# RMS norm inside a fused retention, MLP and gated MLP kernel: means and root rows in two 12-bit parts, diagonals one task earlier

## The chip, the cores and the metric

One core of a Trainium2 chip runs the whole program. The metric is the device time of one execution in microseconds, the median of several runs. The engines of the core work side by side, each through its own list of instructions in order: TensorE (PE; its weight loads are listed as PEld) multiplies matrices into PSUM, ScalarE (ACT) computes functions and copies, VectorE (DVE) does elementwise work, GpSimd (POOL) some of it, and SyncE (SP) issues the transfers. They meet only at semaphores.

## What is computed

Three stages on 1536 tokens of width 512: a retention (linear attention with decay), an MLP with a sigmoid-weighted activation, and an RMS-normed gated MLP. The last one, in which the change lies:

```python
def _moe2_ref(x, w_gate, w_val, w_out, rms_g):
    rms = np.sqrt(np.mean(x * x, axis=-1, keepdims=True) + 1e-06)
    xn = x / rms * rms_g
    g = xn @ w_gate
    silu = g * (1.0 / (1.0 + np.exp(-g)))
    val = xn @ w_val
    return (silu * val @ w_out).astype(np.float32)
```

All of it is in 32-bit floats.

## The kernel before

**Products.** Nearly all large products are made of parts: each factor is split into a high part of 12 bits (a copy by ACT into the type float32r) and the rest (a subtraction by DVE), and `product` (L295) adds three TensorE products, high by high, high by low, low by high. `halves` (L302) makes such a pair. The norm alone still multiplies whole 32-bit floats.

**Tiles and stages.** Tokens lie in three blocks of 512, called 0, 1 and 2 (OTHER, FIRST, LAST). Features lie on the 128 partitions, so a block is 4 tiles of 128 x 512. After the retention comes the first MLP in 48 steps (`STEPS`): step i makes one tile of h (`mlp1_in`, 12 products into one of the two PSUM buffers of the pool `ps_h`), its Silu `g` (`mlp1_act`, ACT, L330), the parts `gh` (ACT) and `gl` (DVE), and one step later 12 products into the four accumulators (`mlp1_out`). `split_in` makes the weight parts `wih`, `wil` two steps ahead into four buffers, `split_out` makes `woh`, `wol` into two; the ACT half waits until TensorE has read the buffer's last content. The second MLP follows as chains (`seven`): products named by output and side, `g0a`, `v0a`, `g0b`, `v0b` and so on, copied and combined by ACT and DVE; finished features go into output products `o`.

**The norm.** When a block is done, `norm_tasks` (L368) gives six tasks, which are handed out one by one between the steps of other work: two with the squares of the four tiles (ACT, L373) and their sum (DVE, L377); one with the means (four TensorE products of the squares with a column of 1/512, L382) and the roots (DVE adds epsilon, ACT takes the square root, L389, DVE the reciprocal and one Newton step, L390 to L394); one with the diagonals (ACT multiplies an identity by each of four columns of roots, L399) and the row of roots (four products of a matrix of ones with them, L407, so that each partition has the root of each token); two in which DVE scales the tiles (L410). Norm 1 is that of block 1 (its means are at 238 us of the trace), norm 2 that of block 0 (262 us), both beside steps 32 to 40 of the first MLP; norm 3, of block 2 (340 us), lies beside the first chains of the second MLP: its squares, means and roots are tasks of the walk through group 0, the rest comes in the walk through group 2.

**What sets the order.** The text of the program gives a first order; while the program is built the instructions of each engine are put into one list by their estimated times, so that neighbours of different tasks mix. A square root and a Silu need different tables of ACT; each change is an instruction `ACT_TABLE_LOAD`. Copies work with either. Beside the norms, ACT and DVE convert the weights of the second MLP from 64-bit words (`qw`, `uw`, L146 to L152); the results are stored to DRAM and reloaded (`w20r`, `w21r`, ...) by transfers on SP's queue.

Of the kernel before, what the change touches and what calls it, by code (L numbers as in the profile page):

```python
# [9 lines left out]
F32 = mybir.dt.float32  # L10
F32R = mybir.dt.float32r
U32 = mybir.dt.uint32
U64 = mybir.dt.uint64
ACTF = mybir.ActivationFunctionType
ALU = mybir.AluOpType
# [3 lines left out]
C = 128  # L19
# [7 lines left out]
T = 512  # L27
NB = NT // T
CPB = T // C
EPS = 1e-6  # L30
# [16 lines left out]
def tile_retention_mlp_swiglu(  # L47
# [19 lines left out]
    nc = tc.nc  # L67
    pool = lambda name, bufs, **kw: ctx.enter_context(tc.tile_pool(name=name, bufs=bufs, **kw))
    const = pool("const", 1)
# [20 lines left out]
    sm_sb = const.tile([128, 12, 1], F32, name="sm_sb")  # L90
    g_sb = const.tile([128, KD], F32, name="g_sb")
    ones = const.tile([128, 128], F32, name="ones")
    mean_w = const.tile([128, 1], F32, name="mean_w")
    pad = const.tile([128, 24], F32, name="pad")
    ident = const.tile([128, 128], F32, name="ident")
    nm = {n: const.tile([128, T // C], F32, name=f"nm{n}") for n in "mqrt"}

    def tmp(name):
        return tmp_p.tile([128, T], F32, tag="tmp", name=name)

    def psum(p, name):
        return p.tile([128, T], F32, tag=p.name, name=name)
# [199 lines left out]
    def halves(hi, lo, src):  # L302
        nc.scalar.activation(out=hi, in_=src, func=ACTF.Copy)  # L303
        nc.vector.tensor_tensor(out=lo, in0=src, in1=hi.bitcast(F32), op=ALU.subtract)  # L304
# [17 lines left out]
    def mlp1_in(i):  # L322
        j, f, _, _ = STEPS[i]
        ps = psum(ps_h, f"h{j}_{f}")
        in_proj(ps, parts.pop(("wi", i)), xt[j])
        return ps
# [41 lines left out]
    def norm_tasks(j, p):  # L368
        x, st = x1[j], {}

        def squares(m):
            sq = tmp(f"sq{j}_{m}")
            nc.scalar.activation(out=sq, in_=x[:, m, :], func=ACTF.Square)  # L373
            if m == 0:
                st["s"] = sq
            else:
                nc.vector.tensor_tensor(out=st["s"], in0=st["s"], in1=sq, op=ALU.add)  # L377

        def means():
            st["ps"] = psum(p, f"mean{j}")  # L380
            for i in range(T // C):
                nc.tensor.matmul(  # L382
                    out=st["ps"][:, i:i + 1], lhsT=st["s"][:, i * C:(i + 1) * C], rhs=mean_w, start=True, stop=True
                )

        def roots():
            m, q, r, t = (nm[n] for n in "mqrt")
            nc.vector.tensor_scalar(out=m, in0=st["ps"][:, 0:T // C], scalar1=EPS, scalar2=None, op0=ALU.add)
            nc.scalar.activation(out=q, in_=m, func=ACTF.Sqrt)  # L389
            nc.vector.reciprocal(out=r, in_=q)  # L390
            nc.vector.tensor_tensor(out=t, in0=r, in1=r, op=ALU.mult)
            nc.vector.tensor_tensor(out=t, in0=t, in1=m, op=ALU.mult)
            nc.vector.tensor_scalar(out=t, in0=t, scalar1=-0.5, scalar2=1.5, op0=ALU.mult, op1=ALU.add)
            nc.vector.tensor_tensor(out=r, in0=r, in1=t, op=ALU.mult)  # L394

        def diagonals():
            st["d"] = tmp(f"diag{j}")
            for i in range(T // C):
                nc.scalar.activation(  # L399
                    out=st["d"][:, i * C:(i + 1) * C], in_=ident, func=ACTF.Copy, scale=nm["r"][:, i:i + 1]  # L400
                )

        def rows():
            st["r"] = psum(p, f"r{j}")
            for i in range(T // C):
                o = slice(i * C, i * C + C)
                nc.tensor.matmul(out=st["r"][:, o], lhsT=ones, rhs=st["d"][:, o], start=True, stop=True)  # L407

        def scale(m):
            nc.vector.scalar_tensor_tensor(  # L410
                out=x[:, m, :], in0=st["r"], scalar=g_sb[:, m:m + 1], in1=x[:, m, :], op0=ALU.mult, op1=ALU.mult
            )

        return [
            lambda: (squares(0), squares(1)), lambda: (squares(2), squares(3)), lambda: (means(), roots()),
            lambda: (diagonals(), rows()),
            lambda: (scale(0), scale(1)), lambda: (scale(2), scale(3)),
        ]

# [294 lines left out]
    for i, (j, f, first, last) in enumerate(STEPS):  # L714
# [9 lines left out]
        ps = mlp1_in(i)  # L724
        next_of(att)
        mlp1_act(i, ps)
        if i:
            mlp1_out(i - 1)
            if STEPS[i - 1][3] and STEPS[i - 1][1] == F1 - 1:
                norm += norm_tasks(STEPS[i - 1][0], ps_t)  # L730
                if STEPS[i - 1][0] == OTHER:
                    norm += x_tasks()
# [61 lines left out]
    mlp1_out(len(STEPS) - 1)  # L794
    reload("w3", 0)
    norm = norm_tasks(LAST, ps_a)
    for g in range(0, F2, 2):
        more = g + 2 < F2
# [6 lines left out]
        n = len(work) - 10  # L805
# [108 lines left out]
```

## Time and profile before

| what | value |
|---|---|
| median of 3 runs | 612.28 us (612.24 to 613.17) |
| the profiled execution | 611.25 us, span 609.4 us |
| PE busy | 596.2 us, 98% of the span, 3354 instructions |
| DVE busy | 443.3 us, 73% |
| ACT busy | 357.0 us, 59% |
| mean granted TensorE clock | 0.994 of full speed |
| chain that ended last | PE 86%, DVE 7%, DMA 3%, ACT 2%, issue 2% |

The span is the time from the first to the last instruction on the core; 1.85 us of the execution lie around it. Busy shares are means over stages with different limits. TensorE's products overlap, so that a product of 512 columns lasts 0.39 us but the next can start 0.23 us later; what counts is the distance of the starts. All times of the rows below are microseconds from the start of the span.

### The profile page before, as it was taken

The numbers are of one execution on the slowest core, as the hardware profiler recorded it, in microseconds if no ns is written. First come the engines' busy times: TensorE is split into PE (matmuls) and PEld (weight loads), VectorE is DVE, ScalarE is ACT, GpSimd is POOL, SyncE is SP. The second block draws the span as 40 slices with busy tenths as digits, with TensorE's granted clock in tenths as the row PEclk, the third lists the DMA queues.
The fourth block names the chain that finished last, engine by engine and source line by source line (L and its number), as shares of the span: only waits on it lengthen the run. The fifth ranks groups of instructions, "written<-read, shape, count | busy, mean of one in ns | idle before, by whom it ended". The sixth has DMA issues, their size and how long they took to land.

```text
span 609.4 us, 9229 instructions
## 1 busy us (share of the span) xinstructions
PE 596.2 (98%) x3354; PEld 496.8 (82%) x3354; DVE 443.3 (73%) x791; ACT 357.0 (59%) x657; POOL 39.1 (6%) x36
## 2 busy tenths in 40 slices
PE   7899999999999999999999999999999999999997
PEld 5678888888878888888887788898988889988885
DVE  2799978777797768889997999374565756655542
ACT  1386847676665558877776875354444536544532
POOL 4516010000022100000000000000000000000000
PEclk8899999999999999999999999999999999999999
DMA  8767652334667545427663132021221366643521
GB/s 335 310 208 272 229 186 94 117 136 155 193 205 233 160 146 159 131 73 227 188 194 118 67 106 104 34 89 51 75 99 46 128 235 220 224 152 104 173 70 69
DMA packets 32733, 93.14 MB, mean 153 GB/s; under 512 B 3888, under 2 KB 3888, under 8 KB 32688
## 3 DMA queue, kind: packets, MB, share of 16 engines
q1 hardware_dynamic: 32688, 92.56, 45.9%
q8 instruction: 26, 0.43, 0.3%
q14 instruction: 19, 0.16, 0.1%
HBM read 73.67 MB, written 18.87 MB: 152 GB/s over the span
## 4 chain that ended last, share of the span: by engine, by line
PE 86%; DVE 7%; DMA 3%; ACT 2%; issue 2%; SPq 0%; POOL 0%; DVEq 0%; ACTq 0%; POOLq 0%
PE acc L298 6%; PE acc L299 6%; PE acc L300 6%; PE h L298 6%; PE h L299 6%; PE h L300 6%; PE o L298 5%; PE o L299 5%; PE o L300 5%; PE sc L225 2%; PE y L257 2%; PE y L247 1%; DVE qw L150 1%; DMA sm_sb<-in_small 1%; DMA w23r<-w23d 1%
## 5 line engine op out<-in xcount | busy, mean ns | idle before, releaser
L299 PE MATMUL acc<-gl,woh 128*128 128x512 f32 x192 | 75.2, 391 | 2.2 <-DVE gl L333 2.2
L298 PE MATMUL acc<-gh,woh 128*128 128x512 f32 x192 | 75.9, 399 | 0.1
L300 PE MATMUL acc<-gh,wol 128*128 128x512 f32 x192 | 74.9, 390 | 0.0
L170 ACT ACTIVATE wih<-w 128x512 fp32r<-128x512 f32 x48 | 30.2, 631 | 65.5 <-PE h L299 56.2
L298 PE MATMUL o<-w3h,gh 128*128 128x512 f32 x144 | 56.2, 390 | 0.0
L299 PE MATMUL o<-w3l,gh 128*128 128x512 f32 x144 | 56.2, 390 | 0.0
L300 PE MATMUL o<-w3h,gl 128*128 128x512 f32 x144 | 56.1, 389 | 0.0
L171 DVE TENSOR_TENSOR wil<-w,wih 128x512 fp32r<-128x512 f32 x48 | 32.8, 689 | 24.9 <-ACT wih L170 24.8
L150 DVE CUSTOM_DVE_ANT_0 qw<-qw,uw 128x1024 uint16<-128x1024 uint16 x68 | 49.8, 733 | 0.6
L146 ACT ACTIVATE qw<-w 128x512 f32<-128x512 f32 x68 | 45.1, 663 | 0.4 <-DMA w<-in_w 0.4
L147 ACT ACTIVATE uw<-w 128x512 uint32<-128x512 uint32 x68 | 45.2, 665 | 0.0
L299 PEld LDWEIGHTS acc<-gl,woh 128*128 128x128 f32 x192 | 36.1, 188 | 10.1 <-DVE gl L333 3.1
L298 PEld LDWEIGHTS acc<-gh,woh 128*128 128x128 f32 x192 | 35.9, 188 | 9.0 <-ACT gh L332 0.6
L300 PEld LDWEIGHTS acc<-gh,wol 128*128 128x128 f32 x192 | 36.0, 188 | 7.5
L170 ACT ACTIVATE woh<-w 128x512 fp32r<-128x512 f32 x48 | 30.2, 630 | 12.5 <-PE acc L299 11.7
L149 DVE TENSOR_SCALAR qw<-qw 128x512 uint32<-128x512 uint32 x68 | 30.4, 448 | 8.8 <-ACT qw L146 8.8
L304 DVE TENSOR_TENSOR gl<-gw,gh 128x512 fp32r<-128x512 f32 x24 | 16.6, 692 | 25.9 <-ACT gh L303 25.9
L333 DVE SCALAR_TENSOR_TENSOR gl<-g,gh 128x512 fp32r<-128x512 f32 x48 | 33.4, 696 | 2.5 <-ACT gh L332 1.0
L171 DVE TENSOR_TENSOR wol<-w,woh 128x512 fp32r<-128x512 f32 x48 | 32.9, 685 | 2.8 <-ACT woh L170 2.7
L300 PEld LDWEIGHTS o<-w3h,gl 128*128 128x128 f32 x144 | 27.0, 188 | 5.6
L303 ACT ACTIVATE gh<-gw 128x512 fp32r<-128x512 f32 x24 | 15.1, 631 | 27.6 <-PE o L299 24.8
L299 PEld LDWEIGHTS o<-w3l,gh 128*128 128x128 f32 x144 | 27.1, 188 | 4.7
(1113 smaller groups left out, 1521.2 us busy)
## 6 DMA issues: line engine op xcount, KB each, us to landing
w<-in_w SPq DMA_DIRECT2D x68, 512.0 KB, 4.4
qk<-in_qk SPq DMA_DIRECT2D x12, 512.0 KB, 6.3
kv<-in_kv SPq DMA_DIRECT2D x12, 512.0 KB, 6.6
g0d<-gs SPq DMA_DIRECT2D x12, 256.0 KB, 2.0
g2d<-gl SPq DMA_DIRECT2D x12, 256.0 KB, 2.1
out<-o SPq DMA_DIRECT2D x12, 256.0 KB, 2.4
gw<-g0d SPq DMA_DIRECT2D x12, 256.0 KB, 2.7
gw<-g2d SPq DMA_DIRECT2D x12, 256.0 KB, 2.7
```

The lines of the kernel that those rows point to most:

```text
L146: nc.scalar.activation(out=q, in_=high.bitcast(F32), func=ACTF.Copy, scale=2.0 ** -112)
L147: nc.scalar.activation(out=t, in_=low, func=ACTF.Copy, scale=2.0 ** -29)
L149: nc.vector.tensor_scalar(out=m, in0=m, scalar1=3, scalar2=None, op0=ALU.logical_shift_left)
L150: nc.vector.tensor_tensor(out=m, in0=m, in1=t, op=ALU.add)
L170: nc.scalar.activation(out=hi, in_=src, func=ACTF.Copy)
L171: nc.vector.tensor_tensor(out=lo, in0=src, in1=hi.bitcast(F32), op=ALU.subtract)
L298: nc.tensor.matmul(out=out, lhsT=ah, rhs=bh, start=first, stop=False)
L299: nc.tensor.matmul(out=out, lhsT=ah, rhs=bl, start=False, stop=False)
L300: nc.tensor.matmul(out=out, lhsT=al, rhs=bh, start=False, stop=last)
L303: nc.scalar.activation(out=hi, in_=src, func=ACTF.Copy)
L304: nc.vector.tensor_tensor(out=lo, in0=src, in1=hi.bitcast(F32), op=ALU.subtract)
L333: nc.vector.scalar_tensor_tensor(out=lo, in0=g, scalar=1.0 / GELU, in1=hi.bitcast(F32), op0=ALU.mult, op1=ALU.subtract)
```

## The change

- The sum of squares `s` is split by `halves` into `sh` and `sl` at the end of the second task (`two`).
- The means are eight float32r products instead of four 32-bit ones: for each group of 128 tokens `sh` and `sl` with `mean_w`, which now has two equal columns, added up in PSUM; the epsilon line reads every second column.
- The row of roots is split too: `nmh` and `nml` (128 x 4 each), and two sets of four diagonals, `diagh` and `diagl`. The row is two float32r products over all 512 columns instead of four 32-bit ones of 128.
- The diagonals move from the fourth task into the third, behind the roots; the fourth task holds only the two products.

```diff
--- before.py
+++ after.py
@@ -90,10 +90,10 @@
     sm_sb = const.tile([128, 12, 1], F32, name="sm_sb")
     g_sb = const.tile([128, KD], F32, name="g_sb")
     ones = const.tile([128, 128], F32, name="ones")
-    mean_w = const.tile([128, 1], F32, name="mean_w")
+    mean_w = const.tile([128, 2], F32, name="mean_w")
     pad = const.tile([128, 24], F32, name="pad")
     ident = const.tile([128, 128], F32, name="ident")
-    nm = {n: const.tile([128, T // C], F32, name=f"nm{n}") for n in "mqrt"}
+    nm = {n: const.tile([128, T // C], F32, name=f"nm{n}") for n in "mqrthl"}
 
     def tmp(name):
         return tmp_p.tile([128, T], F32, tag="tmp", name=name)
@@ -376,16 +376,22 @@
             else:
                 nc.vector.tensor_tensor(out=st["s"], in0=st["s"], in1=sq, op=ALU.add)
 
+        def two():
+            st["sh"], st["sl"] = (tmp(f"s{x}{j}").bitcast(F32R) for x in "hl")
+            halves(st["sh"], st["sl"], st["s"])
+
         def means():
             st["ps"] = psum(p, f"mean{j}")
             for i in range(T // C):
-                nc.tensor.matmul(
-                    out=st["ps"][:, i:i + 1], lhsT=st["s"][:, i * C:(i + 1) * C], rhs=mean_w, start=True, stop=True
-                )
+                for x in ("sh", "sl"):
+                    nc.tensor.matmul(
+                        out=st["ps"][:, 2 * i:2 * i + 2], lhsT=st[x][:, i * C:(i + 1) * C], rhs=mean_w.bitcast(F32R),
+                        start=x == "sh", stop=x == "sl",
+                    )
 
         def roots():
             m, q, r, t = (nm[n] for n in "mqrt")
-            nc.vector.tensor_scalar(out=m, in0=st["ps"][:, 0:T // C], scalar1=EPS, scalar2=None, op0=ALU.add)
+            nc.vector.tensor_scalar(out=m, in0=st["ps"][:, 0:2 * T // C].rearrange("p (i two) -> p i two", two=2)[:, :, 0], scalar1=EPS, scalar2=None, op0=ALU.add)
             nc.scalar.activation(out=q, in_=m, func=ACTF.Sqrt)
             nc.vector.reciprocal(out=r, in_=q)
             nc.vector.tensor_tensor(out=t, in0=r, in1=r, op=ALU.mult)
@@ -394,17 +400,20 @@
             nc.vector.tensor_tensor(out=r, in0=r, in1=t, op=ALU.mult)
 
         def diagonals():
-            st["d"] = tmp(f"diag{j}")
-            for i in range(T // C):
-                nc.scalar.activation(
-                    out=st["d"][:, i * C:(i + 1) * C], in_=ident, func=ACTF.Copy, scale=nm["r"][:, i:i + 1]
-                )
+            halves(nm["h"].bitcast(F32R), nm["l"].bitcast(F32R), nm["r"])
+            for s in "hl":
+                st[s] = tmp(f"diag{s}{j}").bitcast(F32R)
+                for i in range(T // C):
+                    nc.scalar.activation(
+                        out=st[s][:, i * C:(i + 1) * C], in_=ident, func=ACTF.Copy, scale=nm[s][:, i:i + 1]
+                    )
 
         def rows():
             st["r"] = psum(p, f"r{j}")
-            for i in range(T // C):
-                o = slice(i * C, i * C + C)
-                nc.tensor.matmul(out=st["r"][:, o], lhsT=ones, rhs=st["d"][:, o], start=True, stop=True)
+            for s in "hl":
+                nc.tensor.matmul(
+                    out=st["r"], lhsT=ones.bitcast(F32R), rhs=st[s], start=s == "h", stop=s == "l"
+                )
 
         def scale(m):
             nc.vector.scalar_tensor_tensor(
@@ -412,8 +421,8 @@
             )
 
         return [
-            lambda: (squares(0), squares(1)), lambda: (squares(2), squares(3)), lambda: (means(), roots()),
-            lambda: (diagonals(), rows()),
+            lambda: (squares(0), squares(1)), lambda: (squares(2), squares(3), two()),
+            lambda: (means(), roots(), diagonals()), rows,
             lambda: (scale(0), scale(1)), lambda: (scale(2), scale(3)),
         ]
```

The built lists show what this moves. The first place is ACT in norm 1, from the load of the square root's table (L389, L395 in the changed file) on. `nmq` is the square root, `nmr` the finished root, `diag` the diagonals, `wih37` a weight part of step 37, `g33` and `gh33` the Silu of step 33 and its high part, `qw261` and `uw261` a weight conversion; the brackets name the engines waited for. Before:

```order
L389 ACT_TABLE_LOAD
L389 ACTIVATE nmq_107<-nmm_106 128x4 [waits DVE_49]
L330 ACT_TABLE_LOAD [waits DMAHW0_49]
L330 ACTIVATE g33_2590<-h2_1_2577 128x512 [waits PE_49]
L399 ACTIVATE diag1_2620<-ident_105,nmr_108 128x128 [waits DVE_49]
L332 ACTIVATE gh33_2592<-g33_2590 128x512 [waits Activation_49]
L399 ACTIVATE diag1_2620<-ident_105,nmr_108 128x128 x3
L146 ACTIVATE qw270_2630<-w270_64_2417 128x512 [waits DMAHW1_49]
```

Changed:

```order
L395 ACT_TABLE_LOAD
L395 ACTIVATE nmq_107<-nmm_106 128x4 [waits DVE_49]
L170 ACTIVATE wih37_2713<-w15_621 128x512 [waits PE_49]
L303 ACTIVATE nmh_110<-nmr_108 128x4 [waits DVE_49]
L407 ACTIVATE diagh1_2571<-ident_105,nmh_110 128x128 [waits DMAHW0_49,Activation_49]
L407 ACTIVATE diagh1_2571<-ident_105,nmh_110 128x128 x3
L407 ACTIVATE diagl1_2576<-ident_105,nml_111 128x128 [waits DVE_49]
L407 ACTIVATE diagl1_2576<-ident_105,nml_111 128x128 x3
L146 ACTIVATE qw261_2581<-w261_64_2350 128x512 [waits DMAHW7_49]
L147 ACTIVATE uw261_2582<-w261_64_2350 128x512 [waits DMAHW0_49]
L330 ACT_TABLE_LOAD
L330 ACTIVATE g33_2612<-h2_1_2599 128x512 [waits PE_49]
```

`wih37`, the eight diagonals and a conversion now stand between the root and the next Silu; before, only that Silu's table load did. On TensorE the first product of h of step 35 waits for ACT in the new list; it writes the PSUM buffer that `g33` reads. On DVE a subtraction `wil37` stands directly ahead of the last step of `nmr`, and four `scale` operations ahead of `gl33`.

The second place is ACT in norm 2, from `nmq` on; `woh38` is a weight part of step 38, `g37` the Silu of step 37. Before:

```order
L389 ACTIVATE nmq_107<-nmm_106 128x4 [waits DVE_49]
L170 ACTIVATE wih41_2937<-w19_933 128x512 [waits PE_49]
L399 ACTIVATE diag0_2806<-ident_105,nmr_108 128x128 [waits DVE_49]
L399 ACTIVATE diag0_2806<-ident_105,nmr_108 128x128 x3
L146 ACTIVATE qw331_2816<-w331_64_2567 128x512 [waits DMAHW7_49]
L147 ACTIVATE uw331_2817<-w331_64_2567 128x512
L330 ACT_TABLE_LOAD [waits DMAHW0_49]
L330 ACTIVATE g37_2847<-h2_5_2834 128x512 [waits PE_49]
```

Changed:

```order
L395 ACTIVATE nmq_107<-nmm_106 128x4 [waits DVE_49]
L170 ACTIVATE wih41_2965<-w19_935 128x512 [waits PE_49]
L170 ACTIVATE woh38_2908<-w16_704 128x512 [waits PE_49]
L303 ACTIVATE nmh_110<-nmr_108 128x4 [waits DVE_49]
L407 ACTIVATE diagh0_2831<-ident_105,nmh_110 128x128 [waits Activation_49]
L407 ACTIVATE diagh0_2831<-ident_105,nmh_110 128x128 x3
L407 ACTIVATE diagl0_2836<-ident_105,nml_111 128x128 [waits DVE_49]
L407 ACTIVATE diagl0_2836<-ident_105,nml_111 128x128 x3
L146 ACTIVATE qw331_2844<-w331_64_2589 128x512 [waits DMAHW7_49,DMAHW0_49]
L147 ACTIVATE uw331_2845<-w331_64_2589 128x512
L330 ACT_TABLE_LOAD
L330 ACTIVATE g37_2875<-h2_5_2862 128x512
```

`woh38`, which waits for TensorE, moved from behind `g37` to ahead of `nmh`. On TensorE the row's products moved from the middle of step 36's output to h of step 38, and the first product of h of step 39 waits for ACT.

The third place is TensorE in norm 3, from the last products of `g0a` and `v0a` that read the sum `wg0y`, `wv0y` on. `wg0z` belongs to the next pair, which adds to the same PSUM tile after ACT has copied it (`rg`). Before (the row came a group later, between products of `v2a` and `g2b`):

```order
L382 MATMUL mean2_3559<-mean_w_103,sq2_0_3498 128x1 [waits DVE_49]
L382 MATMUL mean2_3559<-mean_w_103,sq2_0_3498 128x1 x3
L587 MATMUL g0a_3445<-xh5_3239,wg0yl_3407 128x512
L587 MATMUL v0a_3458<-xh5_3239,wv0yh_3410 128x512 [waits Activation_49]
L587 MATMUL v0a_3458<-xl5_3240,wv0yh_3410 128x512
L587 MATMUL v0a_3458<-xh5_3239,wv0yl_3411 128x512
L587 MATMUL v0a_3458<-xh5_3239,wv0yh_3410 128x512
L587 MATMUL v0a_3458<-xl5_3240,wv0yh_3410 128x512
L587 MATMUL v0a_3458<-xh5_3239,wv0yl_3411 128x512
L587 MATMUL g0a_3445<-xh3_3243,wg0zh_3414 128x512 [waits Activation_49]
```

Changed:

```order
L387 MATMUL mean2_3591<-mean_w_103,sh2_3561 128x2
L387 MATMUL mean2_3591<-mean_w_103,sl2_3562 128x2
L387 MATMUL mean2_3591<-mean_w_103,sh2_3561 128x2
L387 MATMUL mean2_3591<-mean_w_103,sl2_3562 128x2
L387 MATMUL mean2_3591<-mean_w_103,sh2_3561 128x2
L387 MATMUL mean2_3591<-mean_w_103,sl2_3562 128x2
L596 MATMUL v0a_3486<-xl5_3268,wv0yh_3438 128x512
L596 MATMUL v0a_3486<-xh5_3267,wv0yl_3439 128x512
L414 MATMUL r2_3717<-diagh2_3609,ones_102 128x512 [waits Activation_49]
L298 MATMUL o10_3795<-w3h0_3799,gh0_3522 128x512
L414 MATMUL r2_3717<-diagl2_3614,ones_102 128x512 [waits Activation_49]
L596 MATMUL g0a_3473<-xh3_3271,wg0zh_3442 128x512 [waits Activation_49]
```

The row now stands behind the means with two products of `v0a` between, and `g0a` comes after it. On ACT `wv2yh`, a weight part that reuses the buffer of `wv0y`, stands ahead of the square root's table load, and `rg` moved from ahead of that load to behind the eight diagonals. On DVE `sl` is new between the last addition and the means, and `wv0yl` moved ahead of the first operation that needs the reloaded `w23`, with one of the four operations between that one and `gl47` moved behind it (at 325 us of the old trace).

## Rows read from the trace of the kernel before

**Rows 1.** Busy us by stretch: length, PE, PEld, DVE, ACT, POOL; then clock.

```profile
272.00:322.00 50.00, 50.00 (x222) 41.24 (x221) 49.10 (x83) 38.69 (x68) 0.00 (x0) 1.00 0.64 202
...
362.00:500.00 138.00, 138.00 (x726) 118.80 (x725) 85.98 (x169) 63.58 (x125) 0.00 (x0) 1.00 0.26 93
```

**Rows 2.** Waits of TensorE alone: who <- whom, us in total, times, longest.

```profile
PE acc L299 <- DVE gl L333: 2.2, 2, 1.3
```

**Rows 3.** Line 407, the row of roots: times in ns, first and last start.

```profile
L407 PE MATMUL r<-diag,ones x24: 270/275/377, 244.6 to 353.3; 128*128 128x128 f32 x24
```

**Rows 4.** Timeline of TensorE, norm 1: start, duration, what, tile, count.

```profile
241.62 0.39 PE L298 MATMUL acc<-gh,woh 128*128 128x512 f32 x1
...
244.34 0.39 PE L298 MATMUL h<-xt2h,wih 128*128 128x512 f32 x1
...
245.26 0.40 PE L298 MATMUL h<-xt2h,wih 128*128 128x512 f32 x1
...
245.49 0.83 PE L407 MATMUL r<-diag,ones 128*128 128x128 f32 x6
...
246.39 0.39 PE L300 MATMUL h<-xt2h,wil 128*128 128x512 f32 x1
```

**Rows 5.** Timeline of ACT and DVE, norm 1.

```profile
238.57 1.28 ACT L389 ACT_TABLE_LOAD   x1
...
239.86 0.20 ACT L389 ACTIVATE nmq<-nmm 128x4 f32<-128x4 f32 x1
...
241.82 0.60 ACT L330 ACTIVATE g<-h 128x512 f32<-128x512 f32 x1 [0.45 <-PE h L300]
...
242.60 0.16 DVE L394 TENSOR_TENSOR nmr<-nmr,nmt 128x4 f32<-128x4 f32 x1
...
243.63 0.97 ACT L399 ACTIVATE diag<-ident,nmr 128x128 f32<-128x128 f32 x3
...
244.51 0.64 ACT L146 ACTIVATE qw<-w 128x512 f32<-128x512 f32 x1
...
245.06 0.64 ACT L147 ACTIVATE uw<-w 128x512 uint32<-128x512 uint32 x1
```

**Rows 6.** Timeline of ACT and of TensorE's weight loads, norm 2.

```profile
267.12 1.28 ACT L399 ACTIVATE diag<-ident,nmr 128x128 f32<-128x128 f32 x4 [1.24 <-DVE nmr L394]
...
267.57 0.30 PEld L407 LDWEIGHTS r<-diag,ones 128*128 128x128 f32 x2 [0.51 <-ACT diag L399]
...
270.83 0.60 ACT L330 ACTIVATE g<-h 128x512 f32<-128x512 f32 x1
```

**Rows 7.** Timeline of TensorE, ACT and DVE, norm 3.

```profile
340.12 1.05 PE L382 MATMUL mean<-mean_w,sq 128*128 128x1 f32 x8
...
342.17 1.28 ACT L389 ACT_TABLE_LOAD   x1
...
345.33 0.15 DVE L394 TENSOR_TENSOR nmr<-nmr,nmt 128x4 f32<-128x4 f32 x1
...
346.15 0.50 PE L587 MATMUL v0a<-xh,wv0zh 128*128 128x512 f32 x1 [0.53 <-ACT rv L594]
```

**Rows 8.** Timeline of DVE and TensorE around 325.

```profile
322.75 0.42 DVE L501 TENSOR_TENSOR swg<-w23r 128x256 f32<-128x256 f32 x1 [1.58 <-DMA w23r<-w23d]
...
325.44 0.50 PE L299 MATMUL acc<-gl,woh 128*128 128x512 f32 x1 [1.27 <-DVE gl L333]
```

**Rows 9.** Timeline of TensorE at the start of the program.

```profile
18.41 1.09 PE L247 MATMUL y<-qd,S_sb 64*64 64x128 f32 x16
...
23.49 1.12 PE L282 MATMUL u<-kv,kd 128*64 128x64 f32 x16 [2.51 <-POOL kd L212]
...
24.55 1.97 PE L247 MATMUL y<-qd,S_sb 64*64 64x128 f32 x16
```

**Rows 10.** Busy time at the start and behind 325 (columns as above).

```profile
24.00:26.00 2.00, 2.00 (x26) 1.88 (x24) 1.10 (x3) 0.00 (x0) 0.00 (x0) 0.50 1.02 408
...
326.00:328.00 2.00, 2.00 (x10) 1.66 (x9) 2.00 (x6) 1.53 (x3) 0.00 (x0) 1.00 0.35 137
```

## The prediction

> **What bounds the kernel now.** First the busy time by stage: TensorE works through all 50.00 us of 272 to 322 and all 138.00 us of 362 to 500 [rows 1]. Then the list of who waited for whom, TensorE alone: in the middle of the kernel one wait matters, 1.3 us at 325 for `gl` [rows 2, 8]. So the time is TensorE's row of products, and after 362 no gap is left in which a loss could be made good. ScalarE (ACT) is not full, VectorE (DVE) nearly is (49.10 of 50 us before 322 [rows 1]), and both work strictly in the order of their lists, so the timeline around the three norms (blocks 1, 0 and 2, at 238, 262 and 340 us) decides. It shows that the old chain of roots hardly stops TensorE: in norm 1 the row of roots runs between other products without a wait [rows 4], in norm 2 its weight load stood idle for 0.51 us [rows 6], in norm 3 TensorE stood 0.53 us for the copy `rv`, which ACT made late because two table loads lay ahead of it [rows 7].
>
> My sum is made against the profiled execution, 611.25 us (span 609.4 and 1.85 around it); the median of the runs shown lies 1.03 above it.
>
> **Prices.** A product of 512 columns costs 2.72/12 = 0.227 us of TensorE (from 241.62 to 244.34 twelve start [rows 4]). The six short records of the row take (246.39 - 245.26) - 2 x 0.227 = 0.676, or 0.113 each [rows 4]. Successive 512-wide ACT operations start 0.55 apart [rows 5]; a further diagonal costs 1.28 - 0.97 = 0.31 (four against three [rows 5, 6]); a table load 1.28 [rows 5]. Right behind the load `nmq` starts, at 239.86, when the load ends at 239.85 [rows 5]. The Trainium skill (ScalarE: Activation LUTs, What ACT_TABLE_LOAD costs) adds about 1.4 us of drain to each load; by that the sum below would grow by some 7 us (two loads ahead of the Silu in norms 1 and 2, one in norm 3). The trace does not agree, so that case gets no chance.
>
> **The change on TensorE itself.** The row of roots: 8 short records a norm (24 in all [rows 3]) become two full ones: 0.90 - 0.45 = 0.45 us saved a norm. The means: 8 records before, 8 after, with two columns instead of one. No row shows a 12-bit product so narrow; it lies between 0.113 (same weights, more columns) and 0.227 (full width), 0 to +0.9 a norm; I take 0, since the load of 128 weight columns is the same. Sum: -1.36 us. The added ACT and DVE work (`sh`, `sl`, `nmh`, `nml`, four more diagonals: 0.55 + 0.6 + 0.2 + 0.2 + 1.24 us a norm) would lie beside products if it came early; what it costs is where it stands, place by place below. The moved step issues no transfer. Three more of the 14 `tmp` buffers are taken a norm; where a buffer's last user is a store (`diagh` of norm 1 waits for one) that store was issued some 10 us earlier, so 0. The wider `mean_w` is set by GpSimd before the first product, 0.
>
> **Norm 1.** On ACT the eight diagonals, and behind them `qw`, `uw` and the Silu table load, now stand ahead of `g33`, the Silu of step 33 (order, first place). Before, `g33` ran at 241.82 [rows 5]. Now: `nmr` follows on DVE behind `wil37`, which needs `wih37`, which waits for the last reader in h of step 33. That reader starts two products before 241.62, at 241.17, so it ends near 241.56; `wih37` 241.6 to 242.2, `wil37` to 242.9, `nmr` to 243.0 (242.60 before [rows 5]), `nmh` to 243.25, diagonals 243.3 to 245.7 (8 x 0.31), `qw` and `uw` to 246.75, table load to 248.0, `g33` to 248.6. TensorE starts h of step 34 at 244.34 as before [rows 4]; 12 products and 2 for the row end at 247.5. Then h of step 35 wants the PSUM buffer that `g33` still reads (there are two): 1.1 us of standing. Behind it DVE has four `scale` operations ahead of `gl33`: 0.4 more. +1.55 - 0.45 = **+1.1** (0 if `g33` got ready by 247.5; 1.9 with a slow DVE).
>
> **Norm 2.** On ACT `woh38` now stands ahead of `nmh` (second place). It reuses the buffer of step 36, so it waits for TensorE's second-last product of step 36's output. On the old axis: without the row and its wait that product ends at 267.95; `woh38` to 268.5, `nmh` to 268.7, diagonals to 271.2, `qw`, `uw` to 272.3, table load to 273.55, `g37` to 274.15 (270.83 before [rows 6]). TensorE begins h of step 38 at 268.0, 14 products to 271.2, of which the second row product waits 0.35 for its diagonals; h of step 39 then waits for `g37`: 2.6. Saved: the wait of before, 0.35 of the 0.51 [rows 6], and 0.45. **+2.15** (1.0 to 3.0).
>
> **Norm 3.** Here the cover is thinnest: after the means TensorE has two products left before the row (third place). ACT's `sh` and DVE's `sl` come after the last addition, which lets the means go at 340.12 [rows 7]: 340.1 + 0.6 + 0.7 = 341.4. TensorE runs four products meanwhile and loses 0.25; the means end near 342.4. ACT's `wv2yh` now stands ahead of the Sqrt load and waits for a product behind the means (342.8), so the load starts at 343.35 instead of 342.17 [rows 7], `nmr` comes 1.2 to 1.3 later than 345.33 [rows 7], at 346.6, `nmh` 346.85, four diagonals 348.15. TensorE, free at 342.9, stands 5.3 us. Then one product of `o`, 0.7 for the other four diagonals, 0.3 for the copy `rg`, which ACT makes only behind them. 6.55 in all. Saved: 0.45, and some 1.2 of waits of before (0.53 and its restart for `rv`, the rest for the row's diagonals, which stood one by one between products). **+4.9** (3.5 to 6).
>
> **Between.** The stop at 325 came from DVE waiting 1.58 us for the reload of `w23` and running four operations before `gl47` [rows 8]. Now `wv0yl` fills that wait and `gl47` has one operation less ahead of it: **-0.8** (0 to -1.5). Two transfers on SP's queue change places (`w211d` ahead of `w30r`, `w22r`, `w23r`, and `w21r` earlier); the reload of `w23` was released by DVE, not by them, so I give this nothing.
>
> Sum of the places: 1.1 + 2.15 + 4.9 - 0.8 = +7.35.
>
> **The clock.** At the start TensorE stood 2.51 us before 23.49 and then ran at a granted clock of 0.50, the 1.2 GHz level, for all of 24 to 26; sixteen products took 1.97 us where they take 1.09 [rows 9, 10]. The 1.3 us at 325 left the clock at 1.00 [rows 8, 10]. So the 5.3 us of norm 3 should bring it down, the 2.6 us of norm 2 perhaps. Price: the row shows two us at that level; two to four (an estimate, up to twice the row's) of dense work at half pace lose 1 to 2; I take **+1.7** for norm 3. The Trainium skill (TensorE: Matmul & The Clock Gate, What's actually happening) calls the low level the default, which activity lifts; the trace agrees with its 0.50 at 24 us.
>
> 611.25 + 7.35 + 1.7 = 620.3 for a profiled execution, 621.3 for the median.
>
> **The rivals.**
> 1. Three stops, the clock falls after norm 3 (forecast): 621.3, own range 618.5 to 624.
> 2. Three stops and no fall of the clock: 612.28 + 7.35 = 619.6. For it: products go on in small numbers in norm 3.
> 3. The clock falls after norm 2 too, at its 2.6 us, close to the 2.51 that did it at 23.49 [rows 9]: + 1.7, or 623.0; with a longer low stretch 626.
> 4. Only norm 3 stops: `g33` and `g37` come in time because ACT gets through its waits sooner than I have it. Then norms 1 and 2 give -0.45 and -0.8, and the sum is 612.28 - 1.25 + 4.9 - 0.8 + 1.7 = 616.8.
> 5. Faster: the roots are ready when TensorE reaches the row, as "a step ahead" says. Then 1.36 us of records, 0.35 and 1.2 of waits go: 609.4. It decides at one point, norm 3: from the end of the means to four diagonals there would have to pass 0.45 us of TensorE's work, and the old trace needs 345.33 - 341.17 = 4.2 us for the root alone [rows 7]; in norms 1 and 2 the Silu would have to end by 247.5 and 271.5. I see nothing for it.
>
> **How the numbers follow.** Chances: 1: 0.50; 2: 0.18; 3: 0.17; 4: 0.08; 5: 0.04; nothing that can be told from no change (0.2% is about that limit): 0.03. Faster 0.04, same 0.03, slower 0.93. The time is that of case 1, 621.3. The range must take in 2 and most of 3, the end of my bounds below (1.5 less in the places) and half of 4: 616.8 to 625.5.
>
> **What would show it.** In the profile after: TensorE waiting in h for ACT's Silu (L330) near 248 and 275, each behind a table load; one gap of about 5 us near 345 that ends with the row's product on `diagh`; the granted clock at 0.5 in the microseconds behind it; the row as two records of 512 columns; eight narrow records for the means at about 0.11. Wrong would be: no wait on the Silu (then norms 1 and 2 are cheap), a gap in norm 3 under 3 us (then a chain element is shorter than its row), or narrow records of over 0.2.

## The result, and the profile after

The changed kernel takes 621.47 us (median; single executions 619.17 to 622.29) where the kernel before takes 612.26 on the same chip: ratio 1.0144, 95% interval 1.0124 to 1.0165. Forecast were 621.3 and slower. Its profiled execution took 620.87 us with a span of 619.1, 9.7 more than that of before.

The page's first lines: busy time and instructions, then the shares of the chain that ended last.

```profile
PE 598.0 (97%) x3336; PEld 495.9 (80%) x3336; DVE 446.0 (72%) x797; ACT 363.3 (59%) x675; POOL 33.4 (5%) x36
...
PE 84%; DVE 6%; ACT 4%; issue 2%; DMA 2%; POOL 1%; SPq 0%; DVEq 0%; ACTq 0%; POOLq 0%
```

TensorE has 18 instructions less and 1.8 us more busy time; ACT's share of the chain went from 2% to 4%. Why stands in the list of TensorE's waits (who <- whom, us in total, times, longest), where two lines are new:

```profile
PE r L414 <- ACT diagh L407: 5.3, 1, 5.3
PE h L298 <- ACT g L330: 3.6, 2, 2.5
PE acc L299 <- DVE gl L333: 1.3, 2, 1.0
```

The row waits for the diagonals once, 5.3 us (norm 3); h waits for the Silu twice, 3.6 us in all (norms 1 and 2); the wait for `gl` that [rows 2] shows is smaller.

**Norm 1**, timeline (start, duration, engine, what; the idle time before and its releaser in brackets):

```profile
238.58 0.21 ACT L395 ACTIVATE nmq<-nmm 128x4 f32<-128x4 f32 x1
240.31 0.64 ACT L170 ACTIVATE wih<-w 128x512 fp32r<-128x512 f32 x1 [1.52 <-PE h L299]
...
243.21 1.27 ACT L407 ACTIVATE diagl<-ident,nml 128x128 fp32r<-128x128 f32 x4
...
245.60 1.28 ACT L330 ACT_TABLE_LOAD   x1
246.89 0.60 ACT L330 ACTIVATE g<-h 128x512 f32<-128x512 f32 x1
...
247.54 0.50 PE L298 MATMUL h<-xt2h,wih 128*128 128x512 f32 x1 [1.11 <-ACT g L330]
```

The Silu of step 33 ran at 241.82 in [rows 5]; now it stands behind `wih37`, eight diagonals, a conversion and a table load, runs at 246.89, and TensorE stands 1.11 us in h of step 35. No time passes behind a table load: it starts at 245.60, takes 1.28, and the Silu starts at 246.89.

**Norm 2:**

```profile
267.85 0.64 ACT L170 ACTIVATE woh<-w 128x512 fp32r<-128x512 f32 x1 [2.08 <-PE acc L299]
268.38 0.19 ACT L303 ACTIVATE nmh<-nmr 128x4 fp32r<-128x4 f32 x1
...
273.48 0.60 ACT L330 ACTIVATE g<-h 128x512 f32<-128x512 f32 x1
...
274.13 0.50 PE L298 MATMUL h<-xt2h,wih 128*128 128x512 f32 x1 [2.52 <-ACT g L330]
...
275.16 0.56 PE L299 MATMUL h<-xt2l,wih 128*128 128x512 f32 x1
...
278.80 0.40 PE L300 MATMUL acc<-gh,wol 128*128 128x512 f32 x1
```

`woh38` holds ACT idle for 2.08 us until TensorE has read its buffer, and the Silu of step 37 comes at 273.48 instead of 270.83 [rows 6]. TensorE stands 2.52 us, and the clock falls behind it: the nine products from 275.16 to 278.80 take 3.64 us, at 0.227 they would take 2.04. The busy time by stretch says the same (columns as in [rows 1]):

```profile
276.00:278.00 2.00, 2.00 (x6) 1.60 (x5) 2.00 (x5) 2.00 (x5) 0.00 (x0) 0.50 0.82 248
```

**Norm 3**, timeline and then busy time by stretch:

```profile
345.55 0.39 PE L596 MATMUL v0a<-xh,wv0yl 128*128 128x512 f32 x1
...
346.40 1.28 ACT L395 ACT_TABLE_LOAD   x1
...
349.43 0.17 DVE L400 TENSOR_TENSOR nmr<-nmr,nmt 128x4 f32<-128x4 f32 x1
...
351.20 0.79 PE L414 MATMUL r<-diagh,ones 128*128 128x512 f32 x1 [5.26 <-ACT diagh L407]
...
357.23 0.39 PE L596 MATMUL v0a<-xl,wv0zh 128*128 128x512 f32 x1
```

```profile
348.00:350.00 2.00, 0.00 (x0) 0.00 (x0) 1.69 (x10) 0.34 (x2) 0.00 (x0) 0.50 0.34 131
...
354.00:356.00 2.00, 2.00 (x6) 1.52 (x5) 2.00 (x4) 1.40 (x3) 0.00 (x0) 0.50 0.00 0
```

The row stands 5.26 us for `diagh`, the clock is at 0.50 before it ends, and stays there for the products behind it.

**Around 325** (DVE, then TensorE):

```profile
326.50 0.43 DVE L510 TENSOR_TENSOR swg<-w23r 128x256 f32<-128x256 f32 x1 [0.34 <-DMA w23r<-w23d]
...
327.51 0.68 DVE L333 SCALAR_TENSOR_TENSOR gl<-g,gh 128x512 fp32r<-128x512 f32 x1
...
328.25 0.50 PE L299 MATMUL acc<-gl,woh 128*128 128x512 f32 x1 [0.31 <-DVE gl L333]
```

`gl47` now starts 1.01 us after DVE's first use of `w23` (`swg`). Before, where that use was at 322.75 [rows 8], it was 1.95:

```profile
324.70 0.68 DVE L333 SCALAR_TENSOR_TENSOR gl<-g,gh 128x512 fp32r<-128x512 f32 x1
```

Where the 9.7 us lie can be read from four products that every trace has: the first of the means in norm 1, the first of the means in norm 2, the first of `g0a` (behind 325), the first of `g4a` (behind norm 3). How far each comes later than before, and by how much that grew in between:

| | norm 1's means | norm 2's means | `g0a` | `g4a` | span |
|---|---|---|---|---|---|
| before | 237.95 | 261.61 | 328.07 | 374.71 | 609.4 |
| after | 236.66 | 261.50 | 330.90 | 384.77 | 619.1 |
| later by | -1.29 | -0.11 | 2.83 | 10.06 | 9.7 |
| grown by | start: -1.29 | norm 1: +1.18 | norm 2 and 325: +2.94 | norm 3: +7.23 | rest: -0.4 |

### The profile page after: what moved, and what is told of

It is laid out like the page before. It is cut to its first block, busy times and chain, and to the rows that moved or that the text cites. A ratio compares the mean times of both kernels' runs of the same rounds, so it can differ in the third digit from the quotient of the medians.

```text
span 619.1 us, 9214 instructions
## 1 busy us (share of the span) xinstructions
PE 598.0 (97%) x3336; PEld 495.9 (80%) x3336; DVE 446.0 (72%) x797; ACT 363.3 (59%) x675; POOL 33.4 (5%) x36
## 4 chain that ended last, share of the span: by engine, by line
PE 84%; DVE 6%; ACT 4%; issue 2%; DMA 2%; POOL 1%; SPq 0%; DVEq 0%; ACTq 0%; POOLq 0%
PE acc L298 6%; PE acc L299 6%; PE acc L300 6%; PE h L298 6%; PE h L299 6%; PE h L300 6%; PE o L298 5%; PE o L299 5%; PE o L300 5%; PE sc L225 2%; PE y L257 2%; PE y L247 1%; DMA sm_sb<-in_small 1%; PE g10a L596 1%; PE g8a L596 1%
## 5 line engine op out<-in xcount | busy, mean ns | idle before, releaser
L298 PEld LDWEIGHTS o<-w3h,gh 128*128 128x128 f32 x144 | 27.2, 189 | 4.7
```

The source lines that it names most:

```text
L298: nc.tensor.matmul(out=out, lhsT=ah, rhs=bh, start=first, stop=False)
```

## The experiments

The same reading for each kernel that ran, from its profiled execution (us; the last two columns are the stop of TensorE at 325 for `gl`, and the ratio to the kernel before on the same chip with its 95% interval):

| kernel | start | norm 1 | norm 2 and 325 | norm 3 | stop at 325 | ratio |
|---|---|---|---|---|---|---|
| changed kernel | -1.29 | +1.18 | +2.94 | +7.23 | 0.31 | 1.0144 (1.0124 to 1.0165) |
| undo_third | +0.35 | +1.17 | +3.06 | +0.31 | 0.32 | 1.0049 (1.0030 to 1.0069) |
| parts_only | +1.28 | -0.45 | +4.90 | +0.31 | 0.30 | 1.0065 (1.0040 to 1.0090) |
| move_only | -1.13 | +0.01 | +0.01 | +5.14 | 1.66 | 1.0050 (1.0030 to 1.0071) |
| mean_parts | -0.01 | -0.01 | +2.34 | +0.70 | 2.44 | 0.9995 (0.9978 to 1.0012) |
| fill_gap | +0.78 | +1.20 | +2.69 | +3.43 | 0.30 | 1.0128 (1.0098 to 1.0159) |
| pool_diag | +0.12 | +4.74 | +4.53 | +8.15 | 0.33 | 1.0291 (1.0259 to 1.0324) |
| move_rows | -0.17 | +1.18 | -0.15 | +4.86 | 0 | 1.0088 (1.0064 to 1.0111) |
| nodiag32 | -0.03 | -0.02 | -0.16 | -0.88 | 1.06 | 1.0001 (0.9978 to 1.0025) |
| nodiag_parts | -0.96 | -0.03 | +0.15 | -0.16 | 0.72 | 1.0021 (0.9998 to 1.0044) |
| late_only | +1.05 | -0.04 | +0.43 | +0.05 | 1.75 | 1.0003 (0.9980 to 1.0026) |
| nodiag_late | +1.50 | -0.02 | -0.96 | -0.88 | 0.26 | 0.9959 (0.9944 to 0.9975) |

Up to the means of norm 1 the programs are nearly the same; what differs there, from -1.29 to +1.50, is mostly how one execution differs from another. Ratios rest on 4 to 12 executions each, columns on one, and that one need not be typical: for mean_parts it is the slowest of ten (614.62 us), for nodiag_late the slowest of twelve (610.87), for nodiag_parts the fastest of ten (610.31).

**undo_third: the changed kernel, norm 3 alone put back.**

```
-            lambda: (means(), roots(), diagonals()), rows,
+            lambda: (means(), roots(), diagonals()) if j != LAST else (means(), roots()),
+            lambda: rows() if j != LAST else (diagonals(), rows()),
```

> The changed kernel with one thing undone: in norm 3 alone the diagonals go back into the fourth task. Everything up to 325 us keeps the order of the changed kernel. Theory of places: the 5.3 us stop ahead of the row in norm 3 and the low clock behind it vanish, and with them the 7.1 us by which the offset between the two traces grows there (2.83 at the end of the first MLP, 9.98 at the third pair of chains). 621.5 - 7.2 = 614.3, range 613.3 to 615.5. Rival, the extra work in 12-bit parts costs wherever it stands: only the diagonals' place changes, the work does not, so the time stays above 619.

614.79 us: the stop and the low clock behind it are gone, norm 3 costs 0.31 instead of 7.23 and norms 1 and 2 cost what they did. So the work in parts is not what costs in norm 3, its place is. The 0.31 has a new wait of 0.94 for `qg` at the first `g2a` in it, while the wait for `rv` [rows 7] is gone; mean_parts, which has the same two and keeps the 32-bit row, shows 0.70, and the row in parts saves 0.45 of that.

**parts_only: the move undone in all three norms.**

```
-            lambda: (means(), roots(), diagonals()), rows,
+            lambda: (means(), roots()), lambda: (diagonals(), rows()),
```

> The changed kernel with the move undone in all three norms: parts as in the change, diagonals in the fourth task. On ACT the Silu of step 33 is ahead of the diagonals again, the Silu of step 37 is still behind woh38, nmh and eight diagonals, norm 3 has its row a group later. Theory of places: norm 1 gives back its 1.2 us and keeps the 0.45 saved, norm 2 still stops 2.3 to 2.6 us on the Silu (with 0 to 1.5 for the clock), norm 3 0 to -0.45, 325 us -1.0: 612.3 - 0.45 + 2.4 + 0.8 - 0.3 - 1.0 = 613.8, range 612.6 to 615. Rival, the parts are what costs: 619 or more. Rival, the move is all that costs: 610.3 (three times 0.45 and 1.0 less than before).

616.42 us, more than my range. Norm 1 gives the 0.45 as forecast; norm 3 is as in undo_third; but norm 2 still costs, and more than I had: 4.90 with 325.

```profile
272.98 0.50 PE L414 MATMUL r<-diagl,ones 128*128 128x512 f32 x1 [0.66 <-ACT diagl L407]
275.98 0.80 PE L298 MATMUL h<-xt2h,wih 128*128 128x512 f32 x1 [2.50 <-ACT g L330]
```

TensorE's timeline shows the row's wait of 0.66 and right behind it the wait for the Silu, 2.50; the products behind it run at a clock of 0.50 (its products stand 0.43 apart from 276.57 to 281.69). Taking the diagonals back a task did not help norm 2, because the list built for ACT still has `woh38`, `nmh` and eight diagonals ahead of the Silu of step 37: there the parts alone bring the stop.

**move_only: the kernel before with its 32-bit diagonals in the third task.**

```
-            lambda: (squares(0), squares(1)), lambda: (squares(2), squares(3)), lambda: (means(), roots()),
-            lambda: (diagonals(), rows()),
+            lambda: (squares(0), squares(1)), lambda: (squares(2), squares(3)),
+            lambda: (means(), roots(), diagonals()), rows,
```

> The kernel before with the move alone: one set of four 32-bit diagonals, made in the third task. On ACT in norm 1 the Silu of step 33 stands behind wih37, four diagonals and a conversion (1.4 us sooner than with eight), in norm 2 the order is that of before. In norm 3 seven products, not two, lie between the means and the row, there is no split of the sum, and the Sqrt load is ahead of wv2yh. Theory of places: norms 1 and 2 cost 0, 325 us gives 1.0 to 1.2, norm 3 stops 2 to 3.5 us in one or two pieces, with 0 to 1.7 for the clock, and saves 0.5: 612.3 - 1.1 + 2.8 - 0.5 + 0.5 = 614.0, range 612.5 to 615.5. Rival, the move costs the same with either format: 612.3 + 7.1 = 619.4.

614.67 us. Norms 1 and 2 cost nothing: with four diagonals instead of eight the Silu comes in time. Norm 3 costs 5.14:

```profile
344.73 1.65 PE L407 MATMUL r<-diag,ones 128*128 128x128 f32 x6 [2.94 <-ACT diag L399]
```

The stop is 2.94, inside my 2 to 3.5; behind it the clock is low, and from 344.73 to 350.95 six short records and eleven products take 6.22 us where they would take 0.68 + 2.50: 3.0 more (a wait for `rg` may be in it), against the 0 to 1.7 that I gave it. At 325 there was no gain: the reload of `w23` landed late in this trace (below).

**mean_parts: the kernel before with the means alone in parts** (with `two`, `means` and the epsilon line of the change's diff).

```
-            lambda: (squares(0), squares(1)), lambda: (squares(2), squares(3)), lambda: (means(), roots()),
+            lambda: (squares(0), squares(1)), lambda: (squares(2), squares(3), two()), lambda: (means(), roots()),
```

> The kernel before with the means alone changed: sum of squares in two 12-bit parts, eight float32r products of two columns a norm; row and diagonals stay 32-bit, in the fourth task. Theory: a narrow 12-bit product costs TensorE the same 0.11 us as a short 32-bit record, so 0 a norm; the stop at 325 shrinks by about 1.0 because wv0yl now fills the wait there: 611.3, range 610.6 to 612.4. Rival, narrow products cost up to 0.227 each: +0.9 a norm, 614.

611.24 us, no change. The narrow 12-bit products stand 0.11 apart as the short records did; that term of the sum was right. The profiled execution, the slowest of its ten, lost 2.34 at 325 all the same, though `wv0yl` stands ahead of the reload there too: DVE waited 2.80 for it (below), TensorE stood 2.44, and the clock was at 0.50 behind that.

**fill_gap: the changed kernel with 16 idle products ahead of the row in norm 3.**

```
             st["r"] = psum(p, f"r{j}")
+            if j == LAST:
+                one = lambda n: nc.const_aps.tensor(1.0, [128, n], mybir.dt.bfloat16)
+                for i in range(16):
+                    nc.tensor.matmul(out=st["r"], lhsT=one(128), rhs=one(T), start=True, stop=True)
```

> The changed kernel with 16 idle products (bfloat16 ones, 512 columns, into the row's own PSUM buffer, overwritten by the row) queued behind the last product of v0a in norm 3, so that TensorE does not stand still; nine products of o now stand behind them and ahead of the row, where one stood. 16 x 0.227 + 9 x 0.227 = 5.7 us of work lies in the 5.65 us between the last product of v0a and the row. Theory: the stop still lasts as long, the row still comes then, but the granted clock stays at 1.00: the 13 products that took 6.03 us from 351.20 to 357.23 take 2.95 and wait some 0.7 to 1.0 for diagl and rg, which gives 2.1, and eight products of o are done inside the gap, which gives 1.8. 621.5 - 3.9 = 617.6, range 616.5 to 618.8. Rival, the low clock costs nothing because what follows waits anyway: only the 1.8, 619.7.

In the trace norm 3 costs 3.43 instead of 7.23. TensorE and the clock, in the stretch where the row stood and behind it (compare 348 to 350 and 354 to 356 above):

```profile
348.00:350.00 2.00, 2.00 (x10) 0.89 (x9) 1.81 (x6) 1.70 (x3) 0.00 (x0) 1.00 0.00 0
...
354.00:356.00 2.00, 1.82 (x7) 1.31 (x8) 1.27 (x3) 1.98 (x4) 0.00 (x0) 1.00 0.00 0
```

With the idle products the clock stayed at 1.00. Of the 3.80 saved, 8 x 0.227 = 1.82 are the products of `o` that now lie in the gap; the other 1.98 are what the low clock cost in norm 3 (forecast 1.7). The medians do not show that: 618.67 is 7.9 above before on its chip, 1.3 less than the changed kernel's 9.2. That is nearer to the 1.8 of the rival, by which the low clock costs nothing, than to the 3.9 expected, and the intervals overlap. So the price of the clock in norm 3 rests on the two traces. The mean granted clock of the other executions, 0.991 to 0.994 in three of fill_gap and 0.983 to 0.989 in three of the changed kernel, fits it but does not say where the clock was low.

**pool_diag: the changed kernel with the diagonals on GpSimd.**

```
-                    nc.scalar.activation(
-                        out=st[s][:, i * C:(i + 1) * C], in_=ident, func=ACTF.Copy, scale=nm[s][:, i:i + 1]
+                    nc.gpsimd.tensor_scalar(
+                        out=st[s][:, i * C:(i + 1) * C], in0=ident, scalar1=nm[s][:, i:i + 1].bitcast(F32), scalar2=None, op0=ALU.mult
```

> The changed kernel with the eight diagonals made by GpSimd instead of ACT, still in the third task. Theory: the two waits on the Silu come from the eight diagonals that stand ahead of it on ACT (2.4 us), so g33 and g37 come 2.4 us sooner and TensorE never waits for them in h. In their place TensorE waits for the diagonals in the row, up to 1.7 us in pieces in norms 1 and 2, since the row is placed earlier; no low clock behind norm 2. In norm 3 the 5.3 us stop stays (it is the chain of the root), but rg no longer stands behind the diagonals. 621.5 - 2.2 (norm 2 with its clock) - 0.9 (norm 3) = 618.4, range 616.8 to 620. Rival, the Silu of step 37 is late because woh38 waits for TensorE and the table load comes after: then the wait of 2.5 us on the Silu in norm 2 stays, 620.5.

628.75 us, far out of my range. The list of TensorE's waits has no line for the Silu any more, but two others:

```profile
PE r L414 <- POOL diagh L407: 10.3, 3, 6.4
...
PE r L414 <- POOL diagl L407: 3.0, 2, 1.6
```

and, among the groups of GpSimd's instructions (busy us, mean ns):

```profile
L407 POOL TENSOR_SCALAR diagh<-ident,nmh 128x128 fp32r<-128x128 f32 x12 | 7.8, 662 | 131.8 <-ACT nmh L303 131.8
```

A diagonal takes 0.66 us there, against starts 0.31 apart on ACT. I had taken ACT's price for an operation that no row of GpSimd showed; the wait moved from h to the row and grew. That the wait on the Silu is gone proves little by itself, since TensorE now stands in the row ahead of it. The Silu's own time does show the cause. That of step 37:

```profile
276.00 0.60 ACT L330 ACTIVATE g<-h 128x512 f32<-128x512 f32 x1
```

Counted from norm 2's means (266.47 here, 261.50 in the changed kernel) it starts after 9.53 us instead of 11.98. That is 2.45 less, the 2.4 of the eight diagonals; by the rival, in which `woh38` alone makes it late, it would not have moved. In norm 1 it is 7.75 instead of 10.23.

**move_rows: the change without its first part** (row in parts, diagonals a task earlier).

```
-            lambda: (squares(0), squares(1)), lambda: (squares(2), squares(3), two()),
+            lambda: (squares(0), squares(1)), lambda: (squares(2), squares(3)),
```

The means, `mean_w` and the epsilon line are those of before.

> The changed kernel without its first part: means stay 32-bit and the sum of squares is not split; row in parts and eight diagonals in the third task as in the change. In norm 2 woh38 is not ahead of nmh on ACT, in norm 3 seven products lie between means and row and wv2yh is behind the Sqrt load. Theory of places, my terms of the prediction: norm 1 +1.2 as in the change; norm 2 the stop on the Silu shrinks from 2.5 by the 1.0 that woh38 held nmh, to 1.5, and the clock stays at 1.00; norm 3 the stop is 2.9 (the move alone) + 0.9 (the row needs four diagonals, not one) + 0.3 (nmh) = 4.1 instead of 5.3, the low clock stays; 325 us -0.9. Before + 1.2 + 1.2 - 0.9 + 6.0 - 0.3 = before + 7.2, some 618.5. Rival, the split of the sum and woh38 change nothing, since the chain of the root is all: before + 9.2 as the change.

616.58 us, 4.6 above before on its chip, where I had 7.2. The two waits came out as worked out:

```profile
PE r L408 <- ACT diagh L401: 4.1, 1, 4.1
PE h L298 <- ACT g L330: 2.6, 2, 1.5
```

4.1 in norm 3 and 1.5 in norm 2 (1.10 and 1.52 are the two on the Silu); behind 1.52 the clock stayed at 1.00. So of the 2.5 in norm 2, 1.0 is `woh38`. Of the 5.3 in norm 3, 1.2 go with the split of the sum, but not as I had it: from the end of the means to the row pass 5.9 us here (341.92 to 347.83) and 6.0 in the changed kernel (345.24 to 351.20); what differs is that seven products, not two, are left to run in that time. That `wv2yh` is behind the load here gave nothing in the end: from the end of `nmq` to `nmh` pass 2.9 us, 1.7 in the changed kernel, because DVE now has more other work, `wv2yl` among it, between the steps of the root. Norm 3 cost 4.86, not 6.0, since less of the low clock fell on products: they were back at full pace from 351.72, 3.9 us behind the stop, in the changed kernel 6.0.

**nodiag32, nodiag_parts, late_only, nodiag_late: no diagonals, and a later row.** A diagonal matrix is not needed: the column of roots, read 128 times as the weights, times the identity gives the same row. nodiag32 drops `diagonals` and has:

```
-                nc.tensor.matmul(out=st["r"][:, o], lhsT=ones, rhs=st["d"][:, o], start=True, stop=True)
+                nc.tensor.matmul(out=st["r"][:, o], lhsT=nm["r"][:, i:i + 1].to_broadcast([128, C]), rhs=ident, start=True, stop=True)
```

nodiag_parts does it with `nmh` and `nml`. late_only leaves the diagonals as they were and moves the row from the fourth task to the fifth, away from the root instead of towards it. nodiag_late is nodiag32 with the row in the fifth task:

```
-            rows,
-            lambda: (scale(0), scale(1)), lambda: (scale(2), scale(3)),
+            lambda: None, lambda: (rows(), scale(0), scale(1)), lambda: (scale(2), scale(3)),
```

> The kernel before without any diagonal: the row is a product of the column of roots, read 128 times as the weights, with the identity (four 32-bit products as before, same columns). ACT loses twelve operations. Theory: the waits of the row (0.5 in norm 2) and for rv (0.5 in norm 3) go, norms 1 to 3 cost nothing; at 325 us eight operations of DVE now stand between the reload of w23 and gl47, which may cost 0 to 2 us more there. 611.6 - 1.0 + 0.8 = 611.4, range 609.8 to 613. Rival, weights read from one column load slower: +0.5 or more a norm, 613.5.

> As the one without diagonals, with the roots in two 12-bit parts: eight float32r products of 128 columns a norm. It needs nmh and nml (0.2 us each on ACT and DVE). Theory: eight records of 0.06 to 0.11 us, 0 to 0.4 a norm less on TensorE than the one in 32 bits, and the same at 325 us: 610.9, range 609.3 to 612.7. Rival as there.

> The kernel before with one thing changed: the row of roots is multiplied a task later, in the fifth, and the diagonals stay in the fourth, 32-bit, as before. Opposite of the change's move. Theory: the wait of the row in norm 2 (0.5) goes, at 325 us wv0yl is ahead of the reload of w23 and two operations lie between it and gl47 (0 to 1.0), the rv wait in norm 3 stays: 0.5 to 1.5 less than before, some 611.0 where before takes 612.0. If the kernel without diagonals and with the late row owes its 2.6 us to the late row alone: 2 or more less, 609.6.

> The kernel before without diagonals (row of roots by the broadcast column and the identity, four 32-bit products) and with the row a task later still, in the fifth. Nothing is asked of the root for some 5 us more. Theory: as without diagonals, norms 1 to 3 cost nothing and give back the 0.5 in norm 2 and 0.5 in norm 3; at 325 us wv0yl is ahead of the reload of w23 and three operations, not eight, lie between it and gl47, which gives another 0 to 1.0. 1.0 to 1.8 us less than before on the same chip: about 609.8 where before takes 611.2. Rival, what is saved in the middle is lost to the scatter of the start and of the reload, or to a later wait: within 0.5 of before.

611.04, 612.59 and 612.81 us: none of the three differs from before by more than its interval. nodiag32 did win 0.88 in norm 3 in its trace, but has eight operations of DVE between the reload and `gl47` at 325. In nodiag_parts eight records take 0.9 too, where up to 0.4 less was expected. nodiag_late took 609.32 us, 0.41% less than before (interval 0.25 to 0.56%). That is 2.6 us, more than the 1.0 to 1.8 expected, and some 12 less than the changed kernel. Its three norms hold no wait of TensorE; the row of norm 1:

```profile
251.05 0.39 PE L300 MATMUL acc<-gh,wol 128*128 128x512 f32 x1
251.28 1.05 PE L400 MATMUL r<-ident,nmr 128*128 128x128 f32 x8
252.09 0.48 PE L298 MATMUL h<-xt2h,wih 128*128 128x512 f32 x1
```

Eight records in 0.9 us, the price of before: weights that are one column read 128 times load no slower. In the trace of nodiag_late the gain is 0.88 in norm 3, where the wait for `rv` [rows 7] is gone, and a stop of 0.26 instead of 1.27 at 325. The wait of norm 2 [rows 6] is gone too, but gave nothing: norm 2 and 325 together win 0.96, less than the 1.01 of the stop alone. The rest of the 2.6 no trace shows. Why neither half shows a gain alone is not settled: each half has another order at 325, and the reload another duration.

## Why the prediction was right, and where only in sum

- **TensorE itself:** right. The row is two records of 512 columns; parts_only shows -0.45 in norm 1, mean_parts 0 for the means.
- **Norm 1:** +1.1 forecast, +1.18 measured. The Silu ended at 247.49, on the axis of before 248.78; forecast 248.6. Ahead of `gl33` DVE ran three `scale` operations, not the four that the change's description and the forecast name.
- **Norm 2:** +2.15 forecast. Without the clock 2.94 + 0.96 (what 325 gave back) - 1.60 (the nine slow products) = 2.30. The step holds; move_rows confirms its part `woh38`, pool_diag that of the diagonals.
- **Between:** -0.8 forecast, 0.31 - 1.27 = -0.96 measured, and for the reason forecast: 1.95 - 1.01 = 0.94 less pass from `w23` to `gl47`. All five traces with this order there (changed kernel, undo_third, parts_only, fill_gap, pool_diag) show a stop of 0.30 to 0.33. What the forecast left out is that the reload of `w23` can eat this up: `wv0yl` fills the wait in mean_parts and move_only too, and they stood 2.44 and 1.66. From its issue to DVE's first use pass 5.2 us in the changed kernel (321.31 to 326.50), 5.6 before, 6.7 in move_only, 7.2 in mean_parts. Why it differs, no run here shows.
- **Norm 3:** +4.9 forecast for the place; 7.23 - 1.98 = 5.25 measured. The stop was worked out at 5.3, ended by the row's product on `diagh`; it was 5.26. On the axis of before (2.83 less) the load started at 343.57, forecast 343.35, and the diagonals of the high part were done at 348.3, forecast 348.15.
- **The clock:** here a step failed. I took +1.7 for norm 3 alone and gave the fall behind norm 2 (rival 3) 0.17. It fell there, in this trace and in those of undo_third, parts_only and fill_gap, each at a stop of 2.5 us, and cost 1.60; norm 3 cost 1.98. The term is 3.6, not 1.7. The row I had weighed against it, [rows 8], is a stop of 1.27.
- **The sum:** from the norms to the end the profiled executions differ by 9.7 + 1.29 = 11.0, where I had 9.05. That the median moved by 9.2 is in part luck, by cancelling: before's median lies 1.0 above its profiled execution and the start is worth 1.3 either way. The mechanism is the forecast's with rival 3's clock; the time is the forecast's. In the other kernels too, the sum of the stages and the distance of the medians agree only to 1 or 2 us, in mean_parts to 3.7. The clock has a part in this: the four executions of the changed kernel took 622.29 and 622.07 us at a mean granted clock of 0.983, 620.87 at 0.986 and 619.17 at 0.989. Where those without a trace lost it stays open.
- **Rivals:** 2 (no fall) and 4 (only norm 3 stops) fall by the granted clock and by the waits on the Silu; 5 (roots ready in time) by the 5.26. The Trainium skill (ScalarE: Activation LUTs, What ACT_TABLE_LOAD costs) adds some 1.4 us of drain to each table load; the trace of after does not show it either, neither behind the load (246.89 behind 245.60 + 1.28) nor ahead of it (the conversion before it ends at 245.58).

## What to carry to other kernels

Moving a producer earlier in the program helps only if its consumer waits for it; otherwise what stands behind it on its engine, here a table load and the Silu that TensorE needed next, comes later: the Silu of norm 2 by the 2.45 us of eight diagonals. Look at what the moved instructions stand ahead of in each engine's list, and cost a long stop of a bound TensorE with the low clock behind it. And ask whether the producer is needed: a column read as broadcast weights against the identity gave the row that twelve diagonals were made for, at the same price on TensorE. By itself that saved no time that the runs can tell; together with the later row it did.

## What was not expected of the hardware

The same stop does not always bring the clock down. At the start of the program TensorE stood 2.51 us in both kernels; before, the products behind it ran at a granted clock of 0.50 [rows 9, 10], after at 1.00, as in nodiag_parts:

```profile
23.54 0.69 PE L282 MATMUL u<-kv,kd 128*64 128x64 f32 x16 [2.51 <-POOL kd L212]
24.16 1.09 PE L247 MATMUL y<-qd,S_sb 64*64 64x128 f32 x16
```

Sixteen products took 1.09 instead of 1.97, the sixteen before them 0.69 instead of 1.12. That is the 1.29 by which this execution started ahead, and it may be one reason why executions of one program lie up to 6 us apart (before, on one chip: 609.77 to 616.02). In the middle of the kernel the stops of 2.44, 2.49, 2.50, 2.52, 2.94, 4.08, 5.26 and 6.37 us in these traces had the low clock behind them, single ones of 1.11, 1.27, 1.52, 1.66 and 1.75 did not; in pool_diag two stops of 1.46 and 1.59, which ended at 246.08 and 248.41, did. Of GpSimd: one copy of 128 x 128 with a scale took 0.66 us there; on ACT one lasts 0.40 and the next starts 0.31 later.
